# A Hyena gate behind hedgehog attention on Trainium2: table columns from PSUM, maxima transposed on TensorE, and a new order of the work

## The chip, the cores and the metric

The kernel runs on one core of a Trainium2 chip. The engines are TensorE (PE, matrix products; its weight loads are shown apart as PEld), VectorE (DVE), ScalarE (ACT), GpSimd (POOL) and SyncE (SP), which here only issues DMA transfers. Each engine works off its own queue in order; engines wait for each other by semaphores. The metric is the device time of one execution in microseconds (us), smaller is better.

## The reference

Eight batches, eight heads, a sequence of S = 576 and a head size of 64 are put through a linear attention, and its output through a gate with a long convolution. Cut to what matters:

```python
def phi(x):                                   # x: q or k, [8, 8, 576, 64]
    proj = x @ w_phi                          # 128 features
    proj = proj - max(abs(proj), over features)
    return concat([exp(proj), exp(-proj)])
kv  = k_p^T @ v ;  z = sum over s of k_p
att = (q_p @ kv) / (q_p @ z + 1e-6)
x   = att, heads side by side                 # [8, 576, 512]

x1, x2, x3 = split(x @ w_proj)                # 3 x 512 columns
X2  = rfft(x2, n=576) ;  H = rfft(filter_fft, n=576)
y   = x1 * irfft(X2 * H, n=576) * x3
out = y @ w_out                               # [8, 576, 512], float32
```

The maxima of |proj| are taken row by row. For q the kernel subtracts a row's maximum before the exponential; for k it scales the row of v, and the column of ones that gives z, with the exponential of the maximum instead.

## The kernel before

**An order written out by hand.** The whole kernel is one string of words, `PLAN` (lines 27 to about 205). A word such as `X1e,ACT,4,2@5` is a method with its arguments (an engine, a batch, a piece), behind `@` the first of eight PSUM banks that it uses, behind `#` a slot in a ring of buffers. `run` (line 1015) goes through the words and calls the methods one after the other. So the string is the order of every engine's queue: two words on one engine run in the order of the string, and a word on another engine starts as soon as its operands are there. Nothing is planned at run time.

**A batch.** The words of one batch, in the order of the data:

- `load`/`loadh` (541, 547) bring k, q and v by DMA from POOL's queue. k and q are transposed: for batches 0 and 1 on PE (`tp`, then a copy `tpe`), for the others by DMA (`trh`, 557, SP's queue).
- `Pk` (645) and `Qn` (652) project k and q onto the 128 features, rows on the partitions, and `maxk`/`maxq` (716, DVE) take the maxima of the absolute values. `Pkt`, `Qnt` (659) are the same for the ninth, leftover column group.
- The maxima of q become weights of a product: `mhi` (737, ACT) and `mlo` (742, POOL) split them into two bf16 halves `mh`, which are transposed into `mT`. Batches 0 and 1 do this on PE (`tmp`, which calls `flip` at 584, then a copy `tmpe` out of PSUM); batches 2 to 7 with a DMA transpose (`trm`, 746, SP's queue). `Pq` (673, 679) and `Pqt` project q again, features on the partitions, and subtract the maxima by products with `mT`.
- `ex` (701, ACT) takes the exponentials with both signs. `em` (751, ACT) takes those of k's maxima, and `vs` (757, POOL, in two cases of batches 0 and 1 DVE) scales v with them.
- `KV` (772) forms k_p^T v for half of the heads, `KVe` copies it out, `NE` and `NEt` (791, 800) multiply with q_p, `rc` and `xn` (805, 810, DVE) divide. The result `xn` is transposed into `xT`: on PE in batches 0 and 1 (`txp`), by DMA in the others (`trx`, 829).
- The convolution is done with tables: `fold`, `fold2` (846, 854, POOL) add and subtract the halves of the sequence, `F` (879 to 885) multiplies with the forward table `fwd` into frequencies, `Fe` copies out, `X2` (871) projects, `m12`, `m3` (893 DVE, 904 POOL) multiply with the filter's transform, `I` (963) goes back with the inverse table, `Ie`, `Ip`, `Im` (968, 973) join even and odd parts.
- `X1`, `X3` (910) and their leftovers `X1t`, `X3t` (917) project x; `X1e` copies x1 out, `tm` (953, DVE) multiplies x1 by x3, `ym` (984, mostly POOL) by the convolution, `O` (996) multiplies with w_out, `Oe` copies out and `st` (1007, 1012) stores through SP's queue.

The string weaves several batches into each other: while a batch goes through its gate, the next ones' k and q are projected.

**The head.** Before batch 0 is through, the tables are made on the chip: `gen_rows` to `gen_sin` make the inverse table, `tg` transposes it on PE into PSUM, in two runs (1 and 0) of eight blocks of 128 columns each, and `tge` copies them out into `fwd`, the leading 128 of each 144 columns of a group. The last 16 columns of each group are filled by `gen_left` (line 387): four DVE instructions read 16-column pieces of `fwd` back from SBUF and write them, times a column of signs, to the leftover places. `gen_v`, `gen_h` (POOL) and `F` read them later. The filter is folded by `filt_fold` (459, POOL), transformed by `H` and scaled by `H_ev`.

Of the kernel before, what the change touches and what calls it, by code (L numbers as in the profile page):

```python
# [27 lines left out]
w_load,phi zeros loadh,k,0,0 sintab warm,4@0 gen_rows loadh,k,0,1 gen_cols warm,3@1 loadh,q,0,1  # L28
gen_angles warm,2@0 warm,3@1 ident gen_sin,0 loadh,q,0,0 gen_dc tp,k,0,1@2 warm,2@3 tpe,ACT,k,0,1@2
tp,k,0,0@4 gen_abs w_phi gen_sin,1 tpe,DVE,k,0,0@4 loadh,v,0,0 gen_signs Pk,0,0@6 exptab gen_pads  # L30
maxk,0,0@6 tp,k,0,2@5 tp,k,0,3@4 warm,4@0 tpe,DVE,k,0,2@5 ex,k,p,0,0@6 loadh,k,1,0 tpe,DVE,k,0,3@4
tp,q,0,2@1 ex,k,m,0,0@6 gen_ends,0 tp,q,0,3@0 gen_ends,1 Pkt,0@2 Pk,0,1@4 tpe,ACT,q,0,2@1 maxkt,0@2
gen_selidx Pk,0,3@6 loadh,v,0,1 maxk,0,1@4 tpe,ACT,q,0,3@0 warm,2@1 loadh,k,1,1 exkt,p,0@2
tp,q,0,0@0 tp,q,0,1@1 exkt,m,0@2 maxk,0,3@6 gen_sel em,m,0,0 tpe,ACT,q,0,0@0 Qn,0,3@2 ex,k,p,0,1@4
tpe,DVE,q,0,1@1 warm,3@0 maxq,0,3@2 em,p,0,0 Qn,0,2@0 filt_hold ex,k,m,0,1@4 vs,POOL,m,0,0
filt_load,SP,1 maxq,0,2@0 tp,k,1,0@2 ex,k,m,0,3@6 Pk,0,2@4 maxk,0,2@4 Qn,0,0@0 ex,k,p,0,3@6
tp,k,1,1@3 vs,POOL,p,0,0 filt_load,SP,0 maxq,0,0@0 tpe,ACT,k,1,1@3 Qnt,0@6 tpe,ACT,k,1,0@2 tg,1@3
maxqt,0@6 em,p,0,1 Qn,0,1@0 ex,k,p,0,2@4 vs,POOL,p,0,1 tg,0@2 maxq,0,1@0 Pk,1,1@6 em,m,0,1
# [6 lines left out]
ex,q,p,0,0@2 xn,0,3@6 Pkt,1@4 exkt,p,1@4 rct,0@0 Pq,0,2@2 xnt,0,0@0 exkt,m,1@4 xnt,0,1@0 txp,0,3@6
w_load,proj,2 tp,q,1,3@7 ex,q,p,0,2@2 maxkt,1@4 tp,q,1,2@0 H,0@1 load,v,1 tpe,DVE,q,1,2@0
ex,q,m,0,2@2 NE,0,0@4 tpe,DVE,q,1,3@7 gen_v,POOL H,3@0 rc,0,0@4 H_ev,ACT,0@1 txpe,DVE,0,3@6 NE,0,2@2
xn,0,0@4 Qn,1,2@6 rc,0,2@2 gen_h,POOL H,2@4 xn,0,2@2 H_ev,ACT,3@0 maxq,1,2@6 txp,0,1@5 tv@1
txpe,ACT,0,1@5 H,1@2 w_load,proj,1 tve,ACT,0@1 H_ev,DVE,2@4 Qnt,1@6 H_ev,ACT,1@2 H,4@3 load,k,2
tve,DVE,1@1 txtp,0@0 maxqt,1@6 late Qn,1,1@4 fold,POOL,0,1,0 H_ev,ACT,4@3 txp,0,2@1 txtpe,DVE,0@0  # L50
Qn,1,0@6 maxq,1,1@4 txpe,ACT,0,2@1 Pk,1,0@2 fold,POOL,0,1,1 txp,0,0@0 F,0,1,1@1 txpe,ACT,0,0@0
maxq,1,0@6 Qn,1,3@4 ex,k,m,1,0@2 X1,0,0@0 fold,POOL,0,0,0 maxq,1,3@4 ex,k,p,1,0@2 F,0,3,1@6
fold2,POOL,0,1,0 X1,0,1@7 Fe,ACT,0,3,1@6 maxk,1,0@2 fold,POOL,0,0,1 X1e,ACT,0,0@0 Pk,1,3@4 mhi,1
X3,0,0@6 ex,k,m,1,3@4 X1e,DVE,0,1@7 fold2,POOL,0,0,1 X1,0,2@0 ex,k,p,1,3@4 fold2,DVE,0,1,1 tm,0,0@6
mlo,POOL,1 fold2,POOL,0,0,0 X1t,0@7 em,p,1,0 Fe,DVE,0,1,1@1 X1e,ACT,0,2@0 F,0,3,0@6 load,q,2
maxk,1,3@4 Pk,1,2@2 Fe,ACT,0,3,0@6 tmp,1@1 F,0,2,1@0 ex,k,m,1,2@2 vs,POOL,p,1,0 trh,k,2,0 F,0,0,0@6
# [6 lines left out]
rc,1,0@0 xn,1,0@0 ex,q,p,1,3@6 NE,1,1@2 m1,0,4@5 NEt,1@0 rc,1,1@2 Pq,1,2@6 rct,1@0 xn,1,1@2 NE,1,3@4
ex,q,p,1,2@6 trh,q,2,1 xnt,1,1@0 fold,POOL,1,0,0 I,0,0,0@2 xnt,1,0@0 I,0,2,0@3 rc,1,3@4 Ie,0,0@2#0
xn,1,3@4 Pk,2,1@0 ex,q,m,1,2@6 trh,k,3,1 fold,POOL,1,1,0 X1,0,3@2 maxk,2,1@0 Ie,0,2@3#1 txp,1,0@4
fold2,POOL,1,1,0 NE,1,2@6 ex,k,m,2,1@0 X3,0,1@5 fold2,POOL,1,0,0 rc,1,2@6 xn,1,2@6 load,k,4
txpe,ACT,1,0@4 txp,1,1@3 tm,0,1@5 Qn,2,1@6 ex,k,p,2,1@0 fold,POOL,1,1,1 I,0,2,1@4 maxq,2,1@6
F,1,1,1@5 X1e,ACT,0,3@2 F,1,0,1@0 fold,POOL,1,0,1 txpe,ACT,1,1@3 txp,1,3@1 Im,0,2@4#0 txp,1,2@2
txpe,ACT,1,3@1 Qnt,2@6 F,1,2,1@3 maxqt,2@6 Fe,ACT,1,0,1@0 fold2,POOL,1,0,1 I,0,0,1@1 Fe,ACT,1,2,1@3
Ip,0,2@4#0 X3,0,2@0 txpe,ACT,1,2@2 fold2,POOL,1,1,1 Im,0,0@1#1 Fe,DVE,1,1,1@5 load,v,2 F,1,1,0@4  # L70
Ip,0,0@1#1 Qn,2,0@6 Fe,ACT,1,1,0@4 tm,0,2@0 Qn,2,3@2 w_load,out I,0,3,0@1 maxq,2,0@6 I,0,1,0@5
Ie,0,3@1#1 ym,POOL,0,2 F,1,2,0@4 Ie,0,1@5#0 F,1,3,1@0 Fe,ACT,1,2,0@4 txtp,1@1 maxq,2,3@2
Fe,ACT,1,3,1@0 Pk,2,2@6 Qn,2,2@4 txtpe,ACT,1@1 ym,POOL,0,0 X1,1,0@0 ex,k,p,2,2@6 maxq,2,2@4
F,1,3,0@1 I,0,1,1@2 Fe,ACT,1,3,0@1 I,0,3,1@3 maxk,2,2@6 F,1,0,0@1 X3,0,3@4 Ip,0,3@3#0 ex,k,m,2,2@6
# [6 lines left out]
ex,q,m,2,0@4 m12,1,1@1 vs,POOL,m,2,0 Pq,2,3@2 em,p,2,1 tmt,1@0 X2,1,0@7 ex,q,m,2,3@2 m1,1,4@6
vs,POOL,p,2,1 Pqt,2@4 ex,q,p,2,3@2 m12,1,0@7 KV,2,0@0 exqt,m,2@4 Pq,2,1@2 exqt,p,2@4 KVe,DVE,2,0@0
Pq,2,2@6 m3,POOL,1,1 ex,q,p,2,1@2 trh,q,3,0 KV,2,1@4 ex,q,m,2,1@2 st,0,1 NE,2,0@0 KVe,DVE,2,1@4
ex,q,m,2,2@6 X1,1,3@2 m3,POOL,1,0 rc,2,0@0 xn,2,0@0 trh,q,3,1 ex,q,p,2,2@6 NE,2,1@4 NEt,2@0 rc,2,1@4
X1e,ACT,1,3@2 xn,2,1@4 NE,2,2@6 I,1,0,0@3 rct,2@0 fold,POOL,2,0,0 trx,2,1 rc,2,2@6 xnt,2,1@0
NE,2,3@4 Ie,1,0@3#1 xn,2,2@6 I,1,2,0@2 I,1,2,1@3 rc,2,3@4 load,v,4 Ie,1,2@2#0 xn,2,3@4 X3,1,1@6
fold2,POOL,2,0,0 xnt,2,0@0 trx,2,3 X3,1,3@7 tm,1,1@6 fold,POOL,2,1,0 Ip,1,2@3#1 Pk,3,1@4 trx,2,0
tm,1,3@7 Qn,3,1@0 fold2,POOL,2,1,0 ex,k,m,3,1@4 O,0,0@2 maxq,3,1@0 fold,POOL,2,1,1 ex,k,p,3,1@4
trx,2,2 F,2,1,1@6 I,1,3,0@7 Im,1,2@3#1 I,1,0,1@0 fold,POOL,2,0,1 Fe,ACT,2,1,1@6 maxk,3,1@4 F,2,3,1@1
Ie,1,3@7#0 F,2,1,0@3 F,2,0,0@6 Fe,ACT,2,1,0@3 fold2,POOL,2,0,1 I,1,1,0@7 trh,k,4,0 Im,1,0@0#0  # L90
Oe,ACT,0,0@2#2 Qn,3,0@4 Ip,1,0@0#0 Fe,ACT,2,0,0@6 Qn,3,3@2 maxq,3,0@4 ym,POOL,1,0 Ie,1,1@7#1
Fe,ACT,2,3,1@1 Qnt,3@6 trxt,2 O,0,3@0 maxqt,3@6 fold2,POOL,2,1,1 Qn,3,2@4 maxq,3,3@2 Oe,ACT,0,3@0#3
# [978 lines left out]
```

## Time and profile before

| | us |
|---|---|
| three runs | 313.02, 315.04, 314.55 |
| median | 314.55 |
| the profiled execution's own time | 312.48 |
| its span, from first to last instruction | 310.7 |
| PE busy | 281.2 (91%) |
| DVE busy | 256.4 (83%) |
| POOL busy | 231.4 (74%) |
| ACT busy | 222.4 (72%) |

The profile is of one execution, on which all durations rest. A row of a timeline reads: start, busy time, engine, line, operation, what it writes and reads, and in brackets how long its engine sat idle before it and what ended that. A row of groups adds up all instructions of one line and kind: busy time, mean duration in ns of one, and idle time before them. A PE row's duration runs from start to end of a pipelined instruction, so neighbours overlap. PEclk is the clock that the chip grants PE, 1.00 being full speed; its mean over the span is 0.985. The chain of waits is followed back from the last instruction, at each step to what released it.

### The profile page before, as it was taken

Reading aid. Unit: us, or ns where it says so; the run is one execution under the profiler, and the core shown is the slowest. Engines: PE = TensorE matmul, PEld = TensorE weight load, DVE = VectorE, ACT = ScalarE, POOL = GpSimd, SP = SyncE. Lnnn points to the kernel's source line nnn. Section 1 sums busy time; section 2 is a strip of 40 time slices with the busy share of each in tenths; the row PEclk is TensorE's granted clock in tenths of the full one; section 3 lists DMA queues with packets and bytes.
Section 4 is the critical chain, followed back from the end, with each engine's and each line's share of the span. In section 5 each row is a group of like instructions: output and inputs, shape, how many; then the busy total and the mean of one; then the engine's idle time right before and its main releaser. Section 6 shows DMA issues by size and latency. Waiting matters only on the chain.

```text
span 310.7 us, 9655 instructions
## 1 busy us (share of the span) xinstructions
PE 281.2 (91%) x4004; PEld 175.5 (57%) x4044; DVE 256.4 (83%) x421; ACT 222.4 (72%) x390; POOL 231.4 (74%) x220
## 2 busy tenths in 40 slices
PE   7674999799999997999997999898999999999991
PEld 3453765467557653675465554665548654765540
DVE  5899799979997998399975998699889998579750
ACT  4997799767799587867895489944996589623241
POOL 8889549759499987789696958697298859777340
PEclk9999799979999999999999999999999999999998
DMA  6999975927889999697983686977548940064366
GB/s 92 184 192 148 164 131 89 169 50 116 141 111 159 142 150 153 136 133 146 192 145 77 124 153 111 164 109 143 61 126 98 128 111 3 8 114 92 75 140 161
DMA packets 65707, 38.37 MB, mean 124 GB/s; under 512 B 46016, under 2 KB 60480, under 8 KB 65664
## 3 DMA queue, kind: packets, MB, share of 16 engines
q1 hardware_dynamic: 50800, 21.51, 40.3%
q0 software_dynamic: 14864, 16.26, 35.4%
q8 instruction: 31, 0.51, 0.7%
q14 instruction: 12, 0.10, 0.1%
HBM read 33.75 MB, written 9.44 MB: 139 GB/s over the span
## 4 chain that ended last, share of the span: by engine, by line
PE 70%; DMA 10%; DVE 8%; issue 3%; POOL 3%; ACT 2%; SPq 2%; POOLq 0%; DVEq 0%; ACTq 0%
PE ps L910 14%; PE ps L871 10%; PE ps L996 7%; PE ps L963 6%; PE ps L791 6%; PE ps L772 5%; DMA out_dram<-o 3%; DMA mT<-mh 3%; DMA xT<-xn 2%; PE ps L673 2%; PE ps L879 2%; PE ps L679 2%; PE ps L917 2%; DMA kn<-in_k_dram 2%; PE ps L645 2%
## 5 line engine op out<-in xcount | busy, mean ns | idle before, releaser
L910 PE MATMUL ps<-xT,wproj 128*128 128x512 bf16 x238 | 62.2, 379 | 1.1 <-issue 0.3
L984 POOL TENSOR_TENSOR yT<-cv,x1s 128x576 bf16<-128x576 f32 x30 | 38.5, 1296 | 24.0 <-DVE cv L973 13.4
L716 DVE TENSOR_REDUCE mk<-ps 128x8 f32<-128x1024 f32 (+1 forms) x40 | 43.7, 1111 | 1.3 <-ACT Ekp L701 0.8
L893 DVE TENSOR_TENSOR Y<-ps,AB 128x1024 bf16<-128x1024 f32 x32 | 38.2, 1218 | 7.7 <-PE ps L871 7.3
L716 DVE TENSOR_REDUCE mq<-ps 128x8 f32<-128x1024 f32 (+1 forms) x40 | 43.0, 1109 | 1.5 <-PE ps L652 1.1
L757 POOL TENSOR_TENSOR vm<-vn,vm 128x1152 bf16<-128x1152 bf16 x14 | 30.0, 2153 | 11.2 <-ACT vm L751 11.2
L904 POOL TENSOR_TENSOR Y<-Y 128x1024 bf16<-128x1024 bf16 x16 | 33.8, 2121 | 6.1 <-DVE Y L893 6.1
L701 ACT ACTIVATE Ekm<-ps 128x1024 bf16<-128x1024 f32 x32 | 32.7, 1027 | 6.1 <-PE ps L645 3.9
L757 POOL TENSOR_TENSOR vp<-vn,vp 128x1152 bf16<-128x1152 bf16 x16 | 34.3, 2151 | 3.6 <-ACT vp L751 3.5
L701 ACT ACTIVATE Eqm<-ps 128x1024 bf16<-128x1024 f32 x32 | 32.2, 1032 | 6.7 <-PE ps L679 6.6
L910 PEld LDWEIGHTS <-wproj 128*128 128x128 bf16 x256 | 23.7, 98 | 23.2 <-issue 0.2
L701 ACT ACTIVATE Eqp<-ps 128x1024 bf16<-128x1024 f32 x32 | 32.8, 1034 | 4.7 <-PE ps L679 4.7
L996 PE MATMUL ps<-wout,yT 128*128 128x512 bf16 x134 | 35.2, 379 | 0.6 <-issue 0.2
L701 ACT ACTIVATE Ekp<-ps 128x1024 bf16<-128x1024 f32 x32 | 32.9, 1030 | 2.0 <-PE ps L645 1.4
L963 PE MATMUL ps<-inv,Y 128*128 128x288 bf16 x192 | 31.3, 286 | 1.4 <-ACT o L777 1.3
L871 PE MATMUL ps<-wproj,xf 128*128 128x512 bf16 x120 | 31.4, 380 | 0.5
L777 ACT COPY o<-ps 128x512 f32<-128x512 f32 x27 | 15.9, 591 | 21.4 <-PE ps L996 16.4
L973 DVE TENSOR_TENSOR cv<-es,ps 128x288 f32<-128x288 f32 x64 | 26.4, 446 | 3.0 <-ACT es L968 2.0
L968 ACT COPY es<-ps 128x288 f32<-128x288 f32 x32 | 12.7, 408 | 19.9 <-PE ps L963 17.6
L846 POOL TENSOR_TENSOR od<-xn 128x512 bf16<-128x512 bf16 x16 | 18.4, 1152 | 10.2 <-PE ps L584 7.5
L777 ACT CAST xf<-ps 128x288 bf16<-128x288 f32 x51 | 19.9, 411 | 8.4 <-PE ps L885 8.4
L846 POOL TENSOR_TENSOR ef<-xn 128x512 bf16<-128x512 bf16 x16 | 18.4, 1151 | 8.2 <-DVE xn L810 8.2
(179 smaller groups left out, 678.5 us busy)
## 6 DMA issues: line engine op xcount, KB each, us to landing
out_dram<-o SPq DMA_DIRECT2D x72, 128.0 KB, 2.5
vn<-in_v_dram POOLq DMA_DIRECT2D x7, 576.0 KB, 7.5
kn<-in_k_dram POOLq DMA_DIRECT2D x6, 576.0 KB, 7.5
qn<-in_q_dram POOLq DMA_DIRECT2D x6, 576.0 KB, 6.7
wproj<-in_moe_w_proj_dram POOLq DMA_DIRECT2D x3, 512.0 KB, 6.8
kn<-in_k_dram POOLq DMA_DIRECT2D x4, 288.0 KB, 6.4
qn<-in_q_dram POOLq DMA_DIRECT2D x4, 288.0 KB, 6.0
fl<-in_moe_filter_fft_dram SPq DMA_DIRECT2D x9, 128.0 KB, 6.7
```

The lines of the kernel that those rows point to most:

```text
L701: self.nc.scalar.activation(e, x, AF.Exp, bias=0.0, scale=1.0 if g == "p" else -1.0)
L716: self.nc.vector.tensor_reduce(out=out, in_=src, axis=AX.X, op=ALU.max, apply_absolute_value=True)
L757: self.pick(eng).tensor_tensor(out=t[:, :, :, 0:64], in0=self.at("vn", b)[:, 2 * X:2 * X + 2], in1=t[:, :, :, 64:65].to_broadcast([128, 2, ...
L777: self.nc.scalar.copy(dst, src)
L846: self.pick(eng).tensor_tensor(out=self.at("od" if odd else "ef", b)[:, v].rearrange("p v c x -> p v (c x)"), in0=x[:, v, 0:2, :].rearrang ...
L871: self.mm(self.pb(0), l, w[:, kt, 512:1024], start=(kt == 0), stop=(kt == 3))
L893: self.nc.vector.tensor_tensor(out=self.at("Y", b)[:, i, h, :], in0=self.pb(0).rearrange("p (i x) -> p i x", i=1).to_broadcast([128, 2, 512]),
L904: self.pick(eng).tensor_tensor(out=Y[:, 0:2, :], in0=Y[:, 0:2, :], in1=Y[:, 2:4, :], op=ALU.add)
L910: self.mm(self.pb(0), w[:, kt, f0 + 128 * m:f0 + 128 * m + 128], x[:, kt, :], start=(kt == 0), stop=(kt == 3))
L963: self.mm(self.pb(0, 0, 288), y, inv[:, i, :].rearrange("p (q j t) -> p j q t", q=2, j=9), start=(i == 0), stop=(i == 2))
L984: e.tensor_tensor(out=self.at("yT", b)[:, m, 0:SEQ], in0=self.at("cv", 4 * b + m).rearrange("p j h t -> p (j h t)"), in1=self.at("x1s", b) ...
L996: self.mm(self.pb(0), y[:, kt, 128 * j:128 * j + 128], w[:, kt, :], start=(kt == 0), stop=(kt == 3))
```

## The change

Three things, in one edit.

1. `gen_left` goes. In its place `tgl,1` and `tgl,0` read the 16-column pieces directly from the transposes in PSUM, where `tg,1` and `tg,0` have put them, two DVE instructions each, and write them with the sign into `fwd`. They no longer depend on `tge`.
2. `trm` of batches 2 to 7 goes; `tmp` and `tmpe` do it for all batches: a transpose on PE and a copy out of PSUM, on DVE for batches 0, 2, 4, 5 and 7 and on ACT for 1, 3 and 6.
3. `PLAN` is another string throughout: order, banks, slots, and the engine of some words. Among them `vs,m,1,1`, `fold2` of batch 0 (odd, second pair) and of batch 6, and `ym,6,2` move from DVE to POOL, `yt` of batches 1, 3 and 5 from DVE to ACT, and some copies out of PSUM change between DVE and ACT in both directions. The method `trm` stays in the file and isn't called. All other methods are as they were.

```diff
 PLAN = """
...
-tge,DVE,0,1@2 tp,k,1,2@4 KVe,DVE,0,0@0 ex,k,p,1,1@6 tp,k,1,3@5 loadh,q,1,1 tmp,0@3 tpe,DVE,k,1,3@5
-tmpe,DVE,0@3 ex,k,m,1,1@6 Pq,0,1@0 vs,DVE,m,0,1 ex,q,p,0,1@0 Pq,0,3@6 tge,DVE,0,0@2 filt_fold,POOL,2
-ex,q,m,0,1@0 KV,0,1@2 gen_left tpe,DVE,k,1,2@4 w_load,proj,0 ex,q,m,0,3@6 Pqt,0@0 KVe,DVE,0,1@2
-NE,0,1@4 filt_fold,POOL,1 ex,q,p,0,3@6 Pq,0,0@2 rc,0,1@4 xn,0,1@4 exqt,m,0@0 NE,0,3@6 exqt,p,0@0
...
-trh,q,2,0 tmt,0@7 ex,q,m,1,1@2 KV,1,0@6 vs,DVE,m,1,1 ex,q,m,1,0@0 KV,1,1@2 m3,POOL,0,0 KVe,DVE,1,0@6
...
-exkt,m,2@0 mlo,POOL,2 X2,1,2@3 ym,POOL,0,3 trm,2 X1e,ACT,1,1@2 maxkt,2@0 X3,1,2@2 maxk,2,3@6
...
-mlo,POOL,3 O,1,2@3 load,k,5 trm,3 exkt,p,3@6 xl,ACT,2 X1,2,1@2 maxkt,3@6 ex,k,p,3,0@0 trh,k,4,1
...
+mlo,POOL,0 vs,POOL,p,0,1 tmp,0@7 tg,0@0 KVe,DVE,0,0@4 ex,k,m,1,1@2 tmpe,DVE,0@7 Pq,0,1@4 tgl,1@6
+ex,k,p,1,1@2 tgl,0@0 Pqt,0@6 vs,DVE,m,0,1 load,v,1 ex,q,p,0,1@4 w_load,proj,1 ex,q,m,0,1@4 KV,0,1@2
+tge,DVE,0,0@0 load,k,2 exqt,m,0@6 Pq,0,0@4 filt_fold,POOL,2 exqt,p,0@6 KVe,DVE,0,1@2 ex,q,m,0,0@4
+NE,0,1@6 tge,DVE,0,1@0 Pq,0,3@2 rc,0,1@6 ex,q,p,0,0@4 xn,0,1@6 tp,k,1,2@1 tp,k,1,3@0 tpe,DVE,k,1,2@1
...
+Pq,1,0@4 X3t,0@0 ex,q,p,1,0@4 vs,POOL,m,1,1 X2,0,2@1 tmt,0@0 KVe,DVE,1,0@6 ex,q,m,1,0@4 X2,0,0@0
...
+X1te,ACT,1@7 tmp,2@3 X3,1,1@0 X1e,ACT,1,1@6 m12,1,3@2 vs,POOL,p,2,0 em,m,2,1 ex,k,p,2,3@4 X3t,1@1
...
+maxkt,3@2 ex,k,m,3,0@4 load,q,4 tm,2,0@6 X2,2,0@2 ym,POOL,1,3 ex,k,p,3,0@4 maxk,3,3@0 st,0,0 tmp,3@3
...
-    def gen_left(self):
-
-        x = self.at("fwd").rearrange("p (q w) (e s f) -> p q w e s f", w=2, e=2, s=2)
+    def tgl(self, i):
+
+        p = self.pt(8).rearrange("p (q e s f) -> p q e s f", q=2, e=2, s=2)
+        o = self.at("fwd").rearrange("p (q w) (e s f) -> p q w e s f", w=2, e=2, s=2)
         for e in range(2):
-            for w in range(2):
-                a = 72 * (1 - e)
-                self.nc.vector.tensor_scalar(
-                    out=x[:, :, w, e, :, 128:144], in0=x[:, :, w, e, :, a:a + 16],
-                    scalar1=self.at("cols")[:, w:w + 1], scalar2=None, op0=ALU.mult)
+            a = 72 * (1 - e)
+            self.nc.vector.tensor_scalar(
+                out=o[:, :, i, e, :, 128:144], in0=p[:, :, e, :, a:a + 16],
+                scalar1=self.at("cols")[:, i:i + 1], scalar2=None, op0=ALU.mult)
```

More of the change, by code (lines that the diff above doesn't have):

```diff
@@ L27 @@
 PLAN = """
[L28 to L38, printed above, removed]
@@ L45 @@
[L45 to L56, printed above, removed]
@@ L63 @@
[L63 to L74, printed above, removed]
@@ L81 @@
[L81 to L92, printed above, removed]
@@ new lines @@
+X1e,ACT,0,0@1 maxk,1,0@6 Qn,1,0@4 Fe,ACT,0,2,1@2 fold2,POOL,0,0,0 Pk,1,2@0 Pk,1,3@2 trh,k,2,1
+ex,k,m,1,2@0 fold2,POOL,0,0,1 maxq,1,0@4 F,0,0,1@6 fold2,POOL,0,1,1 X1,0,1@7 ex,k,p,1,3@2 trh,k,2,0
+load,q,2 H_fix F,0,2,0@4 mhi,1 maxk,1,2@0 em,p,1,0 X3,0,0@5 em,m,1,0 fold2,POOL,0,1,0 Fe,ACT,0,0,1@6
+X1e,ACT,0,1@7 mlo,POOL,1 F,0,3,1@6 vs,POOL,p,1,0 maxk,1,3@2 ex,k,p,1,2@0 F,0,1,1@7 Fe,DVE,0,2,0@4
+tmp,1@0 F,0,1,0@1 em,p,1,1 Fe,ACT,0,1,1@7 tm,0,0@5 F,0,3,0@4 Fe,ACT,0,3,1@6 F,0,0,0@7 tmpe,ACT,1@0
+vs,POOL,m,1,0 Fe,DVE,0,3,0@4 X1t,0@6 ex,k,m,1,3@2 X2,0,3@0 X1te,ACT,0@6 em,m,1,1 Fe,ACT,0,0,0@7
@@ new lines @@
+ex,q,m,2,3@4 KVe,DVE,2,0@6 ex,q,p,2,3@4 Pq,2,2@0 m3,POOL,1,1 KVe,DVE,2,1@2 NE,2,0@6 trh,q,3,1
+ex,q,p,2,2@0 NE,2,1@4 rc,2,0@6 xn,2,0@6 X3,1,3@2 ex,q,m,2,2@0 rc,2,1@4 load,v,4 trx,2,0 xn,2,1@4
+NE,2,3@6 NE,2,2@0 fold,POOL,2,1,0 rc,2,3@6 xn,2,3@6 X1,1,3@3 rc,2,2@0 fold,POOL,2,0,0 xn,2,2@0
+NEt,2@4 X1e,ACT,1,3@3 I,1,2,0@6 rct,2@4 trx,2,2 tm,1,3@2 I,1,2,1@7 Ie,1,2@6#1 fold2,POOL,2,1,0
+I,1,0,0@3 Im,1,2@7#0 I,1,0,1@6 fold,POOL,2,1,1 Ie,1,0@3#0 Ip,1,2@7#0 trx,2,1 Pk,3,1@0 xnt,2,1@4
+Qn,3,1@2 ex,k,p,3,1@0 xnt,2,0@4 I,1,3,0@7 fold2,POOL,2,0,0 Ip,1,0@6#1 O,0,0@4 trx,2,3 Im,1,0@6#1
@@ new lines @@
+X3,4,3@2 ym,POOL,4,1 Fe,ACT,5,1,1@6 X1,5,0@3 tm,4,3@2 mhi,6 load,q,7 Ip,4,3@7#0 Pkt,6@0 st,3,1
+X1e,ACT,5,0@3 Im,4,3@7#0 X1,5,2@6 mlo,POOL,6 fold2,POOL,5,0,0 maxk,6,2@4 exkt,m,6@0 F,5,2,1@7
+exkt,p,6@0 load,v,7 Pk,6,0@2 Fe,ACT,5,2,1@7 maxkt,6@0 Pk,6,3@4 ym,POOL,4,3 X1e,ACT,5,2@6 X1,5,1@7
+maxk,6,3@4 ex,k,m,6,0@2 tmp,6@6 X3,5,2@0 tmpe,ACT,6@6 X1e,DVE,5,1@7 ex,k,p,6,0@2 F,5,3,0@1 tm,5,2@0
+F,5,1,0@6 F,5,2,0@7 em,p,6,1 Fe,ACT,5,1,0@6 O,4,1@0 Fe,DVE,5,2,0@7 ex,k,p,6,3@4 maxk,6,0@2 F,5,0,0@6
+X3,5,1@7 Oe,DVE,4,1@0#3 em,p,6,0 ex,k,m,6,3@4 vs,POOL,p,6,0 Pq,6,2@2 Fe,DVE,5,3,0@1 tm,5,1@7
@@ L205 @@
+Im,7,3@4#0 O,6,3@6 tm,7,3@7 ym,DVE,7,3 Oe,ACT,6,3@6#1 O,7,3@7 st,6,3 yt,DVE,7 O,7,1@6 Oe,ACT,7,3@7#2
+st,7,3 O,7,2@7 Oe,DVE,7,1@6#0 O,7,4@0 Oe,ACT,7,2@7#3 st,7,1 O,7,0@1 Oe,ACT,7,4@0#1 st,7,2 st,7,4
+Oe,DVE,7,0@1#2 st,7,0
 """
```

273 lines of the change are left out of this document (150 added, 123 removed).

## The prediction

> **What bounds the kernel now.** I read the busy shares first, then the idle time of TensorE (PE) and what ended it, then the clock around each gap, and last the rows on either side. The shares and the slices:
>
> ```profile
> span 310.7 us, 9655 instructions
> PE 281.2 (91%) x4004; PEld 175.5 (57%) x4044; DVE 256.4 (83%) x421; ACT 222.4 (72%) x390; POOL 231.4 (74%) x220
> ```
>
> PE is busy 91% of the span, so the time is PE's work, plus the idle time between, plus what a lower clock takes. The windows (start and end, length, then the busy time of PE, PEld, DVE, ACT and POOL, PE's granted clock, DMA share, GB/s) split the idle time into head, body and tail:
>
> ```profile
> 0.00:35.00 35.00, 23.99 (x405) 16.33 (x406) 28.75 (x60) 26.71 (x39) 31.34 (x60) 0.95 0.93 150
> 35.00:300.00 265.00, 253.11 (x3585) 157.63 (x3623) 226.49 (x360) 193.20 (x347) 200.11 (x161) 0.99 0.75 119
> 300.00:311.00 11.00, 4.12 (x18) 1.57 (x17) 1.18 (x3) 2.50 (x5) 0.00 (x0) 0.87 0.66 153
> ```
>
> PE is idle 11.0 us (35 − 23.99) in the head, 11.9 in the 265 us of the body and 6.9 at the end. The longest single waits of PE (total, times, longest):
>
> ```profile
> PE ps L791 <- DVE kT L779: 3.4, 1, 3.4
> PE ps L679 <- DMA mT<-mh: 2.4, 1, 2.4
> PE ps L679 <- issue: 2.0, 1, 2.0
> PE ps L772 <- DVE vm L757: 1.9, 1, 1.9
> ```
>
> The first, second and fourth lie at work that the change touches. A gap can cost twice, once as idle time and once as a lower clock behind it. These are the stretches behind the first (31 to 35), the fourth (62 to 66) and around the second:
>
> ```profile
> 31.00:35.00 4.00, 3.88 (x56) 3.35 (x53) 2.09 (x7) 1.94 (x2) 4.00 (x15) 0.58 0.88 120
> 62.00:66.00 4.00, 3.78 (x63) 2.54 (x57) 2.03 (x4) 2.53 (x3) 2.12 (x1) 0.57 0.12 28
> 122.00:126.00 4.00, 1.49 (x27) 0.99 (x26) 1.49 (x2) 1.14 (x4) 3.62 (x2) 1.00 1.25 137
> 126.00:130.00 4.00, 4.00 (x100) 2.56 (x99) 2.25 (x3) 3.92 (x7) 2.25 (x2) 1.00 0.67 184
> ```
>
> At 0.58 for four busy microseconds up to 4 × 0.42 = 1.7 us of work is lost, and at 0.57 also 1.7. Behind the gap at 122 nothing is.
>
> **The change part by part.**
>
> *Leftover columns (gen_left becomes tgl).* This is the first wait. The chain, VectorE (DVE) and GpSimd (POOL) around it:
>
> ```profile
> L387 DVE TENSOR_SCALAR fwd<-fwd,cols 128x64 bf16<-128x64 bf16 x4 | 4.5, 1181 | 0.0
> 24.89 1.62 POOL L459 TENSOR_TENSOR fe<-fl 128x512 bf16<-128x512 f32 x1
> 30.55 0.68 DVE L779 CAST KVs<-ps 128x520 bf16<-128x520 f32 x1
> 11.35 0.20 DVE L437 TENSOR_SCALAR R<-inv 128x64 bf16<-128x64 bf16 x1
> 23.89 0.21 DVE L779 COPY mT<-ps 128x128 bf16<-128x128 bf16 x1
> ```
>
> Four instructions of 64 columns take 1.18 us each from 25.75 on, while POOL runs the fold of the filter from 24.89. The same operation and shape took 0.20 at 11.35: it is held, not long. Behind them on DVE stand a copy of kT and then, at 30.55, the cast of KVs, for which PE waits 3.4 us. No row shows a tensor_scalar that reads PSUM. Bounds: 0.20 (L437; the copy of 128 columns from PSUM took 0.21) and 1.18 (held as now). I take 0.20, since the PSUM copy is the nearest row and the other price has POOL's fold beside it, which in the new order comes behind the four. What is late next: the cast of KVs, 0.68, which nothing hides. So of 3.4 us **2.7** go. ScalarE and POOL stay as busy as they are in the head, so new small waits may appear; half of the clock's 1.7 behind the gap comes back, **0.85**, with 0 and 1.7 as bounds.
>
> [...] The two rows of 0.20 and 1.18 show that the operand's place isn't what costs here.
>
> *Scaling of v in batch 1 (vs,m,1,1) from DVE to POOL.*
>
> ```profile
> 24.02 1.37 DVE L757 TENSOR_TENSOR vm<-vn,vm 128x1152 bf16<-128x1152 bf16 x1
> 57.64 3.62 DVE L757 TENSOR_TENSOR vm<-vn,vm 128x1152 bf16<-128x1152 bf16 x1
> 57.85 0.33 PE L772 MATMUL ps<-vp,Ekp 64*128 64x65 bf16 x10
> 53.70 2.16 POOL L757 TENSOR_TENSOR vm<-vn,vm 128x1152 bf16<-128x1152 bf16 x1
> L854 POOL TENSOR_TENSOR ee<-ef 128x256 bf16<-128x256 bf16 x30 | 19.6, 668 | 0.6
> ```
>
> On DVE it took 3.62 us, against 1.37 at 24.02 for the same shape, and PE waited **1.9** for it. That goes, and half of the clock's loss behind it with it, **0.85** (bounds 0 and 1.7). On POOL it costs 2.16 more, and the fold2 that POOL takes over costs 0.67. Today the second vs of this batch ends at 55.86; with the fold2 ahead of it and the issue of a load that stands between the two today moved behind, which about cancel, it stays there. Today the KV products that need it start at 57.85; in the new order they stand 3.8 us of PE work earlier (by unit prices below), so at 54.05. The new wait for POOL is 1.8 if its work ahead starts when it does today, and 0 if that starts earlier by as much as PE. I take the middle, **+0.9**.
>
> *Transposes of the maxima (trm by DMA becomes tmp on PE), batches 2 to 7.*
>
> ```profile
> 115.67 0.25 POOL L742 TENSOR_TENSOR mh<-mq,mh 128x36 bf16<-128x36 f32 x1 [0.56 <-ACT mh L737]
> 115.94 8.65 DMA mT<-mh
> mT<-mh SPq DMA_TRANSPOSE x6, 2.6
> 22.77 0.68 PE L584 MATMUL ps<-idn,kn 128*128 128x128 bf16 x9
> 23.28 0.22 PE L584 MATMUL ps<-idn,mh 128*128 128x128 bf16 x1
> ```
>
> Six transfers leave SP's queue. Five landed well before their use; batch 3's took 8.65 us against a median of 2.6 and is PE's wait of 2.4 until it lands at 124.6. That **2.4** goes. No clock comes back here (1.00 on both sides). The new transposes cost PE between 0.08 each (nine in 0.68 us) and 0.22 (one alone): 0.45 to 1.3 us for six, and I take **+0.5**, as PE's neighbours overlap. The copies out, 0.21 on DVE and somewhat more on ScalarE, lie beside PE.
>
> The price of the edit is a wait: tmp stands in PE's own queue, so all PE work behind it waits for the last maximum and POOL's mh. How long mh lags behind the last projection of q, at two batches of today:
>
> ```profile
> 78.41 0.39 PE L652 MATMUL ps<-wphi,qT 64*128 64x128 bf16 x8
> 84.85 0.25 POOL L742 TENSOR_TENSOR mh<-mq,mh 128x36 bf16<-128x36 f32 x1
> 145.00 0.40 PE L652 MATMUL ps<-wphi,qT 64*128 64x128 bf16 x8
> 147.10 0.26 POOL L742 TENSOR_TENSOR mh<-mq,mh 128x36 bf16<-128x36 f32 x1
> 170.56 1.10 PE ps L963 x9
> 150.68 1.73 PE ps L910 x8
> 175.08 0.55 PE ps L652 x16
> 94.74 1.16 PE ps L772 x72
> ```
>
> The lag is 6.3 us in batch 2 (78.80 to 85.10) and 2.0 in batch 4. The last four rows, of the chain, give the price of PE work at a stretch: 0.86 for four matmuls of 512 columns, 0.37 for three of 288, 0.27 for eight of Q or K, 1.16 for a KV word. With them I counted the PE work that the new order puts between the last Q projection of a batch and its tmp: 3.7, 9.5, 5.5, 9.1, 5.3, 5.2 and 7.1 us for batches 1 to 7. At a lag of 2.0 no wait follows; at 6.3 in every batch the shortfalls add up to 2.6 + 0.8 + 1.0 + 1.1 = 5.5. At the middle, 4.1, only batch 1 is short, by 0.4. I take **+0.5**.
>
> *The rest of the new order.* The words are else the same. Priced by these groups, PE's sum is unchanged to 0.5 us, DVE loses 6 us, POOL gains 5 and ScalarE 1. With PE at 91% the engines' sums alone are worth nothing. In the tail the same five output tiles follow the last product:
>
> ```profile
> out_dram<-o SPq DMA_DIRECT2D x72, 128.0 KB, 2.5
> ```
>
> Their twelve stores of 2.5 us to landing stand in the same places, so I cost the tail at nothing. The wait of 2.0 at L679 for issue and the smaller gaps in the body have no cause that the edit removes; the new order draws its own, bounded by today's rest of the body, 11.9 − 2.4 − 1.9 = 7.6 us. I keep them at the same size.
>
> **Sum.** Against the profiled execution's 312.48: −2.7 − 0.85 (head) − 1.9 − 0.85 + 0.9 (batch 1) − 2.4 + 0.5 + 0.5 (maxima) = 305.7. The median of the runs shown, 314.55, is 2.1 above the profiled execution, and I carry that over: 307.8, so **308 us**.
>
> **Rivals.**
>
> 1. *A transfer takes the place of the one removed, and nothing is won.* X's projections need the DMA transposes of xn. These are the rows:
>
> ```profile
> L810 DVE TENSOR_TENSOR xn<-ps,r 128x512 bf16<-128x512 f32 x32 | 21.6, 685 | 0.7
> L829 SPq DMA_TRANSPOSE xT<-xn x24: 1190/1257/2147, 101.3 to 279.7; - x24
> 101.26 7.41 DMA xT<-xn
> ```
>
> The new order leaves 8.8, 9.2, 9.7 and 9.3 us of PE work between the last NE and the first X in batches 2, 5, 6 and 7, where today it is 9.9, 11.5, 10.3 and 14.3. The way takes 0.69 + 1.26 + landing. At 7.41 that is 9.4, short by 0.6 and 0.2 only. If landings are as long as the maxima's 8.65, it is 10.6, short by 1.8, 1.4, 0.9 and 1.3: 5.4 us, so 305.7 + 5.4 + 2.1 = **313**. Against it stands that this 7.41 is the longest of them on today's chain, and that no wait of PE for xT is among the longest.
>
> 2. *The maxima come late (slower).* DVE's queue or POOL's delays mh, and tmp holds PE. In batches 3, 5 and 6 a lag 2 us over the distance costs 2 + 1.7 each, since a gap of 1.9 was followed by the low clock: 305.7 − 0.5 + 11.1 + 2.1 = **318**. It decides once the lag passes about 7.3 where the distance is 5.3 (6.3 was seen). With delays in the new order's other waits it goes to 321.
>
> [...]
>
> 3. *The change doesn't do what it says in the head.* The four tgl are held at 1.18 as well, PE waits as before and its clock falls: 308 + 3.5 = **311.5**. For it: the new order puts POOL's scaling of v (a vs of batch 0) a few words ahead of the four, so POOL may still be at work beside them. Against it: between that and POOL's folds stand issues of loads.
>
> 4. *All comes back*: both clocks whole, no wait for POOL and no late maximum: 305.7 − 1.7 − 0.9 − 0.5 + 2.1 = **305**.
>
> **How the numbers follow.** Chances: forecast 0.45, rival 1 0.13, rival 2 0.22, rival 3 0.09, rival 4 0.11. A difference of 1% is about what a measurement of this kernel tells from none: below 311.4 is faster, above 317.7 slower. Faster gets the forecast, rival 4 and half of rival 3, 0.60; slower most of rival 2, 0.21; the same the rest, 0.19. The range goes from 302.5 (rival 4 with the 2.1 not carried over) to 318.5 (rival 2 at its price, with half of its chance left above).
>
> **What would show each step.** Right: the L387 rows gone and four tensor_scalars of about 0.2 us from PSUM in their place, PE's wait at L791 under 1 us; the head to 35 us with a clock above 0.95; no wait for vm on DVE, and at most 1 to 2 us for POOL's; no DMA of mT, and waits at L584 for mh under 1 us in sum. Wrong: waits of 2 us at L584 for mq or mh, waits at L910 for DMA xT, tgl at 1 us, or new stretches with the clock near 0.57 in the body.

## The result, and the profile after

| | before | after |
|---|---|---|
| median beside each other | 314.8 (313.02 to 315.82) | 303.94 (303.85 to 303.99) |
| profiled execution | 312.48 | 303.95 |
| its span | 310.7 | 301.8 |

The ratio is 0.966, 95% interval 0.962 to 0.971: the changed kernel is faster by 3.4%. A ratio here compares the executions within 1.5% of the fastest of their kernel and a median takes all of them, so a ratio isn't quite the quotient of two medians. In three further sets of runs the median of the kernel before was 311.3, 311.9 and 310.5, with single runs from 307 to 319; the changed kernel, run again in one of them, had 303.35 (302.86 to 304.27) against 311.88, a ratio of 0.976 (0.972 to 0.981). So the kernel before varies by several microseconds and the changed one by about one, and the gain is 2.4 to 3.4%, depending on which executions of before are in the set.

The page of the profile after, its first lines:

```profile
span 301.8 us, 9680 instructions
PE 279.9 (93%) x4008; PEld 174.5 (58%) x4050; DVE 250.5 (83%) x418; ACT 222.0 (74%) x395; POOL 234.9 (78%) x224
```

The windows, for head, body and tail (the body ends 9 us earlier):

```profile
0.00:35.00 35.00, 26.63 (x463) 18.02 (x465) 28.82 (x70) 29.03 (x45) 30.60 (x55) 1.00 1.08 179
35.00:291.00 256.00, 249.23 (x3530) 154.94 (x3568) 219.86 (x347) 191.18 (x349) 204.32 (x170) 1.00 0.72 118
291.00:302.00 11.00, 4.03 (x18) 1.58 (x17) 1.79 (x4) 1.83 (x4) 0.00 (x0) 0.85 0.62 144
```

PE's idle time is 8.4 us in the first 35 us (11.0 before), 6.8 in the body (11.9) and 7.0 at the end (6.9): 7.6 us less in all. PE's busy time is 1.3 less; together that is the 8.9 of the span. The clock reads 1.00 in the whole head and body, where before it had two stretches at one half. The longest waits of PE that are left:

```profile
PE ps L585 <- ACT Ekp L702: 2.5, 3, 1.4
PE ps L313 <- DVE cols L335: 1.1, 1, 1.1
PE ps L792 <- issue: 1.0, 3, 0.6
PE ps L646 <- ACT kT L778: 0.8, 1, 0.8
PE ps L911 <- DVE o L780: 0.8, 1, 0.8
```

Of the four waits of before, three are gone and the third (2.0 us for issue, ahead of the products with `sel`) is down to 0.3. Behind 35 us lie only most of the third row, the fifth, and 0.56 us of the first. The new forms at their places, from the timeline of VectorE and GpSimd in the head, and of GpSimd in batch 1:

```profile
22.99 0.72 DVE L388 TENSOR_SCALAR fwd<-ps,cols 128x64 bf16<-128x64 bf16 x4
23.62 1.58 DVE L758 TENSOR_TENSOR vm<-vn,vm 128x1152 bf16<-128x1152 bf16 x1
21.82 2.15 POOL L758 TENSOR_TENSOR vp<-vn,vp 128x1152 bf16<-128x1152 bf16 x1
53.45 2.14 POOL L758 TENSOR_TENSOR vm<-vn,vm 128x1152 bf16<-128x1152 bf16 x1
```

The four tensor_scalars take 0.72 us together, all of it while GpSimd is at work (21.82 to 23.97). The fourth scaling of batch 1 ends on GpSimd at 55.6, and PE doesn't wait for it.

To see where the time came from, I took for each batch the start of its divisions (L810, after: L811) and subtracted the PE work that the order puts ahead of them, at the prediction's unit prices; the least of the four pieces of a batch is shown. A difference between two columns is what was gained up to there, as an estimate: between two orders it is no better than the unit prices.

| divisions of batch | before | after | gained | old order, tgl alone | old, vs alone | old, tmp alone | old, all three | new, DMA transposes back |
|---|---|---|---|---|---|---|---|---|
| 0 | 12.6 | 10.0 | 2.6 | 9.6 | 12.4 | 16.4 | 11.0 | 10.2 |
| 1 | 17.5 | 12.0 | 5.5 | 12.7 | 15.6 | 20.0 | 13.0 | 12.3 |
| 3 | 22.0 | 14.9 | 7.1 | 16.7 | 19.7 | 22.4 | 15.5 | 22.2 |
| 5 | 27.0 | 16.8 | 10.2 | 23.0 | 24.4 | 28.3 | 21.5 | 24.6 |
| 7 | 29.2 | 19.3 | 9.9 | 24.9 | 26.6 | 32.1 | 25.6 | 27.5 |
| span | 310.7 | 301.8 | 8.9 | 306.0 | 308.0 | 314.0 | 307.4 | 309.0 |

The head and batch 1 gave 5.5 us, batch 3 about 2 more, batches 4 and 5 some 3 more, and the end takes about 1 back.

### The profile page after: what moved, and what is told of

It is laid out like the page before. It is cut to its first block, busy times and chain, and to the rows that moved or that the text cites. A ratio compares the mean times of both kernels' runs of the same rounds, so it can differ in the third digit from the quotient of the medians.

```text
span 301.8 us, 9680 instructions
## 1 busy us (share of the span) xinstructions
PE 279.9 (93%) x4008; PEld 174.5 (58%) x4050; DVE 250.5 (83%) x418; ACT 222.0 (74%) x395; POOL 234.9 (78%) x224
## 4 chain that ended last, share of the span: by engine, by line
PE 71%; DVE 11%; ACT 6%; issue 4%; DMA 3%; POOL 2%; SPq 1%; DVEq 0%; ACTq 0%; POOLq 0%
PE ps L911 15%; PE ps L872 11%; PE ps L997 8%; PE ps L964 6%; PE ps L773 5%; PE ps L792 5%; DVE mq L717 4%; PE ps L674 3%; PE ps L918 2%; DVE mk L717 2%; PE ps L680 2%; PE ps L886 2%; PE ps L880 2%; PE ps L646 2%; PE ps L653 2%
## 5 line engine op out<-in xcount | busy, mean ns | idle before, releaser
L911 PE MATMUL ps<-xT,wproj 128*128 128x512 bf16 x243 | 63.0, 379 | 1.8 <-DVE o L780 0.8
L985 POOL TENSOR_TENSOR yT<-cv,x1s 128x576 bf16<-128x576 f32 x31 | 39.3, 1280 | 18.6 <-PE ps L872 6.7
L758 POOL TENSOR_TENSOR vm<-vn,vm 128x1152 bf16<-128x1152 bf16 x15 | 32.1, 2150 | 3.3 <-ACT vm L752 3.3
L872 PE MATMUL ps<-wproj,xf 128*128 128x512 bf16 x116 | 30.7, 380 | 0.7 <-issue 0.2
L778 ACT CAST x1s<-ps 128x512 bf16<-128x512 f32 (+1 forms) x36 | 19.6, 555 | 15.1 <-PE ps L911 8.1
L969 ACT COPY es<-ps 128x288 f32<-128x288 f32 x32 | 12.4, 403 | 23.0 <-PE ps L964 18.7
L954 DVE TENSOR_TENSOR x1s<-ps,x1s 128x512 bf16<-128x512 f32 x32 | 21.9, 686 | 2.1 <-PE ps L911 1.8
```

The costliest lines, as they stand in the source:

```text
L758: self.pick(eng).tensor_tensor(out=t[:, :, :, 0:64], in0=self.at("vn", b)[:, 2 * X:2 * X + 2], in1=t[:, :, :, 64:65].to_broadcast([128, 2, ...
L778: self.nc.scalar.copy(dst, src)
L872: self.mm(self.pb(0), l, w[:, kt, 512:1024], start=(kt == 0), stop=(kt == 3))
L911: self.mm(self.pb(0), w[:, kt, f0 + 128 * m:f0 + 128 * m + 128], x[:, kt, :], start=(kt == 0), stop=(kt == 3))
L985: e.tensor_tensor(out=self.at("yT", b)[:, m, 0:SEQ], in0=self.at("cv", 4 * b + m).rearrange("p j h t -> p (j h t)"), in1=self.at("x1s", b) ...
```

## The experiments

My theory: the gain is the three named stalls and the low clock behind them, each worth its price in any order. The rival: the new order as such is the gain, and the three edits alone bring little, since other waits take the place of those removed. The first four runs make one edit each, and then all three, in the old order. They ran in one set, in which the kernel before had 311.28 (308.38 to 317.05, 19 runs).

**The leftover columns alone.**

```diff
-... tge,ACT,1,0@3 ... tge,DVE,0,0@2 ... KV,0,1@2 gen_left
+... tge,ACT,1,0@3 tgl,1@3 ... tge,DVE,0,0@2 tgl,0@2 ... KV,0,1@2
```

> The old order with the leftover columns alone taken from PSUM (two instructions right behind each pair of copies of the table). If the named stalls are the gain, whatever the order: four tensor_scalars of about 0.18 us in place of 1.18, TensorE's wait of 3.4 us ahead of NE falls to about 0.7, and the stretch at half clock behind it (31.6 to 35.0 us) is gone: 2.7 + 1.7 = 4.4 us less, a ratio of 0.986. If the new order is the gain and this edit isn't: under 1 us less, since the next wait (the folds of the filter, or ScalarE) takes the place of the one removed.

Measured: 305.77 (302.93 to 307.81), ratio 0.979 (0.971 to 0.987). The wait ahead of NE is gone from PE's waits, and the two others that I had named stand at the top, 2.4 us for the transfer and 1.9 for the scaling of v, as before. Two of the four instructions now run beside the first of GpSimd's folds, as gen_left did:

```profile
25.66 0.40 DVE L392 TENSOR_SCALAR fwd<-ps,cols 128x64 bf16<-128x64 bf16 x2
24.36 5.87 POOL L464 TENSOR_TENSOR fe<-fl 128x512 bf16<-128x512 f32 x4
```

From PSUM they take 0.24 us each, 0.40 together, where gen_left's first two took 0.80 and 1.32 from SBUF beside the same folds. 5.5 us less where 4.4 were expected: this edit keeps its price without the new order.

**The scaling of v alone.**

```diff
-vs,DVE,m,1,1
+vs,POOL,m,1,1
```

> The old order with the one scaling of v in batch 1 moved from VectorE to GpSimd. If the named stalls are the gain: the wait of 1.9 us and the half clock behind it (1.7) go, up to 1 us of new waiting for GpSimd comes: about 2.7 us less, 0.991. If GpSimd is as late as VectorE was: no change.

Measured: 310.05 (305.96 to 315.45), ratio 0.993 (0.988 to 0.998). PE's wait at the place falls from 1.9 to 0.7 us (for GpSimd's half), and the profiled execution (309.76) has no low clock behind it. 1.2 us less by the medians, 2.2 by the ratio and 2.7 by the profiled executions (which are of two sets), 2.7 expected.

**The maxima alone.** `trm` of batches 2 to 7 is dropped, and `tmp`, `tmpe` stand at the best free bank behind the split, 8 to 10 us of PE work behind the last Q projection (4 and 5 in batches 5 and 6).

```diff
-trm,3
+tmp,3@1 tmpe,ACT,3@1
```

> The old order with the maxima of batches 2 to 7 transposed on TensorE, each as far behind the last Q projection as a free bank allows (4 to 10 us of TensorE's work). If the named stalls are the gain: the wait of 2.4 us for the transfer in batch 3 is gone and six transposes cost 0.5: about 2 us less, 0.994, and no wait of TensorE for the maxima. If the transposes hold TensorE's queue in place of the transfer: no gain, up to 1 us more.

Measured: 316.06 (315.51 to 317.87), ratio 1.016 (1.010 to 1.022): slower. The table shows two causes. In batch 3 it gains what was expected (2.4 of lateness between the divisions of batches 1 and 3, 4.5 before). In batches 4 to 6 it gives that back to new or longer waits of PE (the wait for `o` was 1.3 before):

```profile
PE ps L768 <- DVE fwd L775: 5.7, 1, 5.7
PE ps L959 <- ACT o L773: 3.0, 1, 3.0
PE ps L768 <- DVE vm L753: 1.9, 1, 1.9
PE ps L580 <- DVE Y L889: 1.6, 2, 0.9
PE ps L906 <- DMA xT<-xn: 1.5, 1, 1.5
```

The fourth row is tmp itself, in batches 2 and 5, and it doesn't wait for the maxima, which are ready 3 us and more ahead: it waits for its PSUM bank, from which VectorE still reads. The first row is the other cause, and it isn't the edit's: it lies at 25.8 us, ahead of every word that was changed.

```profile
24.50 6.64 DVE L753 TENSOR_TENSOR vm<-vn,vm 128x1152 bf16<-128x1152 bf16 x1
24.98 4.93 POOL L455 TENSOR_TENSOR fe<-fl 128x512 bf16<-128x512 f32 x4
31.51 0.79 DVE L383 TENSOR_SCALAR fwd<-fwd,cols 128x64 bf16<-128x64 bf16 x4
```

Here VectorE's scaling of v began half a microsecond ahead of GpSimd's four folds and ended 1.2 us behind the last of them: 6.64 us for what took 1.37 at the same place before. gen_left, which came behind them, took 0.2 us for each of its four. In the trace of before it was the other way round, and PE lost 3.4 us. The head of the old order is a race, and a head start alone doesn't decide it: in the seven traces of the old order the scaling begins 0.3 to 1.1 us ahead of the folds and takes 1.35 to 2.32 us in six of them (1.35 with the shortest head start) and 6.64 in this one, with 0.5. All four runs of this kernel took over 315 us, and why it falls this way there, with the same words, stays open.

**All three in the old order.**

> The old order with all three edits. If the named stalls are the gain: the sum, about 9 us less, 0.971, and the new order as such is worth 2 us. If the new order is the gain: 3 us less or fewer, 0.99 or above, and the new order as such is worth 8 us.

Measured: 308.24 (306.51 to 309.42), ratio 0.991 (0.987 to 0.995). That is 3.0 us less by the medians, where the theory had 9 and the rival 3 or fewer: the rival's figure. tgl alone had given 5.5 in the same set, so in the old order the other two edits take some back. But the rival's account doesn't hold alone either: up to batch 3 the old order with the three edits is as good as the new one (15.5 against 14.9 in the table), and behind it loses 5.7 us. Its longest waits:

```profile
PE ps L969 <- ACT o L783: 2.8, 1, 2.8
PE ps L590 <- DVE Y L899: 1.6, 2, 0.9
PE ps L916 <- DMA xT<-xn: 1.3, 1, 1.3
```

The next four runs belong together (before: 311.88): the changed kernel again, and three that undo one part in the new order.

**The changed kernel again.**

> The changed kernel once more, beside the kernel before on the same chip as the runs that undo a part of it. If the stretches at half clock are what makes the kernel before vary, this one, with no long gap, again varies by a few tenths of a microsecond around 304, while the kernel before varies by several.

Measured: 303.35 (302.86 to 304.27). It varies by 1.4 us, a little more than expected; before varied by 7.4 in the same set.

**The leftover columns from SBUF again.**

```diff
-tgl,1@6 ... tgl,0@0 ... tge,DVE,0,1@0
+... tge,DVE,0,1@0 gen_left
```

> The new order with the leftover columns again read back from SBUF, behind the last copy of the table, beside GpSimd's folds. If GpSimd's work holds VectorE's instructions on SBUF: up to 1.2 us for each of the four, NE's divisions queued behind them, 3 to 5 us more than the changed kernel. If the source in PSUM is not what counts: four instructions of 0.2 us, under 1 us more.

Measured: 303.54, 304.63, 309.22 and 309.48. The profiled execution is the first of them, VectorE and GpSimd there:

```profile
27.53 0.68 DVE L393 TENSOR_SCALAR fwd<-fwd,cols 128x64 bf16<-128x64 bf16 x4
28.58 3.74 POOL L465 TENSOR_TENSOR fe<-fl 128x512 bf16<-128x512 f32 x3 [1.67 <-issue]
```

GpSimd's folds begin 0.4 us behind the four, which run unhindered, at 0.68 us together, and the time is that of the changed kernel. By that, reading PSUM brings nothing in itself where the folds come behind; it pays where the instructions run beside them, as in the old order. Two of the four executions are 5 to 6 us longer; they left no trace, and what made them longer stays open.

**The scaling of v on VectorE again.**

```diff
-vs,POOL,m,1,1
+vs,DVE,m,1,1
```

> The new order with the scaling of v in batch 1 back on VectorE, at the same place. If two engines on SBUF hold each other: 2 to 4 us for the instruction in place of 1.4, TensorE waits 1 to 2 us and may lose 1.7 to the clock: 1 to 4 us more. If it was only a matter of the old order: no difference.

Measured: 305.21 (303.93 to 305.46), 1.9 us more than the changed kernel. VectorE and GpSimd at the place:

```profile
51.97 2.76 DVE L753 TENSOR_TENSOR vm<-vn,vm 128x1152 bf16<-128x1152 bf16 x1
51.37 2.14 POOL L753 TENSOR_TENSOR vp<-vn,vp 128x1152 bf16<-128x1152 bf16 x1
```

VectorE's instruction ends at 54.7, 1.2 us behind the end of GpSimd's (53.5): held, then worked off. PE waited 0.6 us behind it. Another 0.7 lies in the head, ahead of the edit: the scaling of v that is on VectorE in both kernels took 2.31 us there (1.58 in the changed kernel), and PE waited 1.1 for it (0.4). So this trace shows 0.6 of the 1.9 us as the edit's own.

**The DMA transposes of the maxima again.**

```diff
-mlo,POOL,3 ... tmp,3@3 ... tmpe,ACT,3@3
+mlo,POOL,3 trm,3
```

(so for batches 2 to 7)

> The new order with the maxima of batches 2 to 7 again transposed by DMA, right behind their second half. If a long landing was the only cost of the transfer: 0 us more in most executions and 2 to 3 in those with a landing of 8 us. If SP's queue or the other transfers pay for the six transposes: 1 to 4 us more throughout, with waits for xT or for out.

Measured: 312.02 (310.71 to 315.95), 8.7 us more than the changed kernel: in the new order this one edit is worth the whole gain. PE's longest wait, the issue, and the transfers between 105 and 121 us (median us to landing):

```profile
121.02 0.48 PE L674 MATMUL ps<-mT,sel 64*128 64x128 bf16 x8 [4.73 <-DMA mT<-mh]
114.19 1.36 SPq L741 DMA_TRANSPOSE mT<-mh  x1
out_dram<-o SPq DMA_DIRECT2D x6, 128.0 KB, 5.3
kn<-in_k_dram POOLq DMA_DIRECT2D x1, 576.0 KB, 7.8
qn<-in_q_dram POOLq DMA_DIRECT2D x1, 576.0 KB, 7.9
kT<-kn SPq DMA_TRANSPOSE x3, 6.4
mT<-mh SPq DMA_TRANSPOSE x1, 6.8
```

A transfer of one tile of 128x128 bf16 (32 KB) lands after 6.8 us, while three transposes of k, two loads and the stores are under way in the same stretch; that they are the reason is likely, but no run here takes them away. The table gives 7.3 us of lateness by the divisions of batch 3: 4.7 of wait, 1.7 for a stretch at half clock behind it, and under 1 besides. In the old order PE waited for the same batch's transfer too: 2.4 us in the kernel before, 2.4 and 2.7 in the runs with one edit, and not at all in one further trace (the folds moved, below), where it landed after 5.0.

The landing isn't what got worse: it took 8.65 us in the kernel before. The room did. There PE had work for 6.3 us between the issue (115.94) and the first product that needs `mT`; here it wants it at 116.3, 2.1 us behind the issue (114.19). The new order was drawn with the transpose on PE, so it leaves no room for a transfer. 8.7 us is the price of the DMA way in this order; a new order drawn around the transfers wasn't tried.

**The DMA transposes in all batches but 3.**

> The new order with the maxima by DMA again in batches 2, 4, 5, 6 and 7, and on TensorE in batch 3. If batch 3's transfer, which shares the DMA engines with two transposes of k, a load of 576 KB and stores, is the cost of the DMA way: most of the 8.7 us that all six cost come back, 305 to 306. If the six cost about the same each: 310 to 311.

Measured, in a third set (before: 310.5, for this run and those below): 305.82 (304.23 to 308.05), ratio 0.985 (0.977 to 0.993). By the ratios, 0.985 between 1.001 and 0.976, one batch on TensorE gives two thirds of it back, and its profiled execution (304.23) is within 0.3 of the changed kernel's. In that trace PE waits for one of the other five, 0.7 us in batch 6; by execution the five cost 0 to 4 us. Batch 3 is the one with the least room, so this run doesn't tell a long landing from a short distance.

**The folds moved, gen_left as it was.**

```diff
-gen_left ... filt_fold,POOL,1 ... rc,0,3@6 ... filt_fold,POOL,0
+gen_left ... rc,0,3@6 filt_fold,POOL,1 filt_fold,POOL,0
```

> The old order with gen_left as it was, reading SBUF, and GpSimd's folds of the two tables moved behind the division of batch 0's second piece. If GpSimd's work is what holds the four instructions: 0.2 us each in place of 1.18, TensorE's wait of 3.4 us ahead of NE falls under 1 and the half clock behind it goes: 2.7 to 4.4 us less in the head, of which the filter's products may take back 1 to 2, since the folds end some 5 us later. If reading SBUF itself costs 1.18: gen_left and the wait stay, and the folds only come later: the same time or up to 3 us more.

Measured: 311.03 (308.56 to 313.53), ratio 1.003 (0.998 to 1.008), no difference. The edit did not do what I meant: GpSimd's queue holds nothing between the load and the folds that waits for VectorE, so they began about where they did before, at 25.05, and gen_left took 0.8 to 1.3 each beside them. A place in the string is an order, not a time.

**Four more instructions on SBUF, in the changed kernel.**

```diff
+probe: 4 x tensor_scalar, spare tile (SBUF) <- fwd (SBUF), 128x64, ahead of tgl,1
```

> The changed kernel with four more VectorE instructions of gen_left's shape, from SBUF to a spare tile in SBUF, ahead of those that read PSUM, where GpSimd is scaling v (21.8 to 24.0 us). If GpSimd holds what reads SBUF: the four take over 1 us together, up to the end of GpSimd's instruction, and those from PSUM behind them stay at 0.18 each. If it is the folds alone that hold, or nothing does at this place: 0.2 each, 0.8 in all.

Measured, one execution: 304.61. The tile's instructions (duration in ns: least, median, longest), then VectorE and GpSimd at the place:

```profile
L391 DVE TENSOR_SCALAR prb<-fwd,cols x4: 227/296/650, 23.9 to 24.9; 128x64 bf16<-128x64 bf16 x4
23.88 1.23 DVE L391 TENSOR_SCALAR prb<-fwd,cols 128x64 bf16<-128x64 bf16 x4
25.03 0.71 DVE L383 TENSOR_SCALAR fwd<-ps,cols 128x64 bf16<-128x64 bf16 x4
22.06 2.15 POOL L761 TENSOR_TENSOR vp<-vn,vp 128x1152 bf16<-128x1152 bf16 x1
24.14 0.81 POOL L545 DMA_DIRECT2D vn<-in_v_dram  x1
```

They came 1 us later than planned, so GpSimd's scaling covers only the first 0.3 us. Two of the four took 0.23, one was held to 0.37 beside the end of the scaling, one to 0.65, up to the end of GpSimd's issue of a load at 24.95. The sum of 1.23 fits "held", though not as cleanly as meant. The clearer pair is above, in the old order: 0.80 and 1.32 us from SBUF beside the folds, 0.24 each from PSUM beside the same fold.

**Six output buffers in the old order with all three edits.**

```diff
-'o': 4
+'o': 6      (slots 0 to 5 in turn)
```

> The old order with all three edits and six buffers for the output tiles in place of four. If the wait of 2.8 us at 208 us (a product with the inverse table that waits for a bank which ScalarE copies out late, because its output buffer is still being stored) is the buffers' doing: it goes, and 2 to 3 us with it, about 305.5; so much of the new order's worth is then the place of its stores. If the copy is late for another reason: no change against 308.2.

With six buffers some of the output tiles that the kernel stores are wrong, for a reason that stays open, so only its times and waits are read: the instructions and their order are those of the run with all three edits. Measured: 304.97 (302.94 to 310.18), against 308.24 in the earlier set; by the profiled executions the span is 304.6 against 307.4. ScalarE's wait for the stores, in the run with four buffers and in the kernels before and after:

```profile
ACT o L783 <- DMA out_dram<-o: 4.3, 2, 3.8
```

```profile
ACT o L777 <- DMA out_dram<-o: 4.6, 3, 2.3
```

```profile
ACT o L778 <- DMA out_dram<-o: 1.8, 1, 1.8
```

With six it is gone, and so is PE's wait of 2.8. So about half of what the new order is worth behind batch 3 (2.8 of 5.7 us) is that its copies of the output come when a buffer is free: in the old one a copy sits on ScalarE behind a late store, and the bank that PE wants behind the copy.

## Why the prediction was right, and where not

**The sum.** 305.7 was forecast for the profiled execution and 303.95 measured; 308 for the median, and 303.94 measured. The direction and the range held; the forecast gain was 4 us too small, and rival 4, all comes back, at 305, was the nearest. The sum is nearer than its terms. The wait ahead of NE (0.3), the clock (1.7), the wait for GpSimd (0.9) and the other gaps of the body (1.4) all gave more than I took; PE's busy time gave some back (see the clock).

**Leftover columns.** Right in kind and size: 0.18 us each (0.20 taken), and NE's wait 0.4 in place of 3.4. But I named the wrong instruction behind gen_left. These rows are of the kernel before:

```profile
30.15 0.48 DVE L779 COPY kT<-ps 128x640 bf16<-128x640 bf16 x1
30.68 0.19 PE L791 MATMUL ps<-KVs,Eqp 128*128 128x65 bf16 x1 [3.36 <-DVE kT L779]
```

NE starts as the copy of kT ends, half a microsecond before the cast of KVs ends, and the half of KVs that it reads had been copied at 22.89. What it waited for was its PSUM bank (4), which kT's copy empties. So the 0.68 that I left standing for the cast had no ground, and 3.0 went, not 2.7. That the 5.5 us up to batch 1 agree with the 5.4 forecast for head and batch 1 is partly luck: behind it stand larger terms for the wait and the clock and none for GpSimd, and small new waits, since PE's idle time in the first 35 us fell by 2.6 only. Right too that GpSimd holds the old form; wrong that the nearest danger, GpSimd's scaling ahead of the four (rival 3), would matter: the form that reads PSUM isn't held. Side by side the four took 0.72 us from PSUM (after) and 0.68 from SBUF with the folds behind them (leftover columns from SBUF again), so the edit's worth is only that it isn't held.

**The clock.** The mis-sized term. I took half of each loss back (0.85 twice); all of it came back, 1.7 twice: at the distances that the same shapes have at full rate, the matmuls of the two stretches would have taken an estimated 1.7 us less in each. PE's busy time fell by only 1.3, though, so 2.1 us of other busy time came in, the six transposes among it; what the rest is, no run here shows. My reading that an idle time of 1.9 halves the clock and one of 2.4 doesn't was of gap lengths, where the place in a fixed grid decided (below).

**Scaling of v.** The wait of 1.9 went; of the new wait of 0.9 for GpSimd nothing came (the lower bound): the second scaling of the batch, which I had left at 55.86, ends at 51.4, 4.5 us earlier, while the products that need it start at 55.76, only 2.1 earlier than before.

**Maxima.** The 2.4 of batch 3 went, and the waits in PE's queue came out as sized, by luck: 0.56, in batch 1, where 0.5 was forecast with batch 1 as the short one. But mh was ready at 47.2 there and tmp starts at 48.3: it waited for its PSUM bank, from which ScalarE was still reading an exponential's input. mh was there in time in all of batches 1 to 7, so my price, a late mh, was paid nowhere, and rival 2 had no place. What I had wrong is what the edit is worth in this order: 8.7 us, not 1.4. With the transfer, PE would have waited 4.7 us in batch 3, with the low clock behind it, since the new order asks for `mT` 2.1 us behind the issue and the old one 6.3. Priced against the trace of before, a term says what goes from the old kernel, not what the new one would lose without it. Rival 1 feared the long landing for xT's transposes: in the new order no wait of PE for them shows among the longest; in the old one there is one of 1.3 to 1.6, in the three traces with tmp and in one without it.

**The rest of the order.** "The same size" was nearly right as a sum: 7.6 us of other idle time in the body became 6.2 (6.8 with the 0.56 ahead of tmp). But it hid a trade: the waits of 2.0, 1.3 and 0.9 behind 160 us are all but gone and smaller ones came. That isn't luck of the draw: with the old order the three edits together end 4 to 6 us later.

**From the profiled execution to the median.** The 2.1 us that I carried over were wrong. They belong to the variation of before, which the changed kernel hardly has (303.95 and 303.94).

## What to carry to other kernels

A small transfer can land late: the six of the kernel before took 2.2 to 8.65 us, the longest with a load of 576 KB, a transpose of k and four stores issued while it was under way; that these are the reason is likely, but no run here takes them away. What it costs is set by the work that the waiting engine has between issue and use (6.3 us hid most of it, 2.1 didn't). In the new order a product of 0.22 us on a TensorE that is 93% busy was the cheaper transpose; in the old order it gained in batch 3 and lost behind it. Two engines that hold each other made a race here whose outcome differed by microseconds between kernels with the same words at that place (1.35 to 2.32 us for the scaling of v in six traces, 6.64 in one); in every trace here the four that read PSUM stayed out of it. Gaps of TensorE that leave some 1.8 us of a stretch of the grid idle go first: half rate followed 1.82 and 1.86 us, at an estimated 1.7 us on top of the gap, and once did not follow 2.03.
